# Ten byte offsets, modulo 512, for the weight buffers of a linear-attention and MLP kernel

## The chip, the cores and the metric

The kernel runs on one core of a Trainium2 chip. The metric is device time in microseconds of one execution: 1016.26 us before the change, the median of 2 runs (1016.14 to 1016.39).

## What is computed

The reference first runs attention with random features (8 batches, 8 heads, 576 tokens, head size 64, 128 features), and then a two-layer network over the 4608 tokens, 512 wide, with 2048 hidden units and softplus between the layers:

```python
def phi(x):
    proj = np.einsum('bhsd,md->bhsm', x, omega)
    h = proj - np.sum(x * x, axis=-1, keepdims=True) / 2.0
    h = h - np.max(h, axis=-1, keepdims=True)
    return np.exp(h) / np.sqrt(m)
q_p, k_p = phi(q * scale), phi(k * scale)
kv, z = einsum('bhsm,bhsd->bhmd', k_p, v), sum(k_p, axis=2)
x = einsum('bhsm,bhmd->bhsd', q_p, kv) / (einsum('bhsm,bhm->bhs', q_p, z)[..., None] + 1e-06)
x = x.transpose(0, 2, 1, 3).reshape(4608, 512)
h = x @ w_in                                        # 512 -> 2048
g = maximum(h, 0.0) + log1p(exp(-abs(h)))
out = g @ w_out                                     # 2048 -> 512
```

## The kernel before

The network takes nearly all of TensorE's time. Its tokens go in ten blocks: two of 256 tokens and eight of 512, the last of which (the `rest`) holds what the other blocks left over. The hidden units go in 16 chunks of 128 (`fc` 0 to 15). The numbers are split into a high and a low part, both float32r, and each product is made of three matmuls. Layer 1 (L923 to L925) multiplies a chunk of `w_in`, which is loaded into the array as the stationary operand (128 columns, 512 bytes of each partition), with 512 tokens of `xh` or `xl`, which stream through it (the moving operand, 2048 bytes of each partition). Layer 2 (L952 to L954) is the other way round: 128 tokens of `gh` or `gl` are loaded, and 512 columns of the chunk of `w_out` stream. A weight load is an instruction of its own in the trace (PEld), and the load for the next matmul runs while the present one streams.

Between the layers ScalarE and VectorE make softplus and the split (L929 to L946). The attention of later batches runs between the matmuls of the network: features (L399, L424), key-value sums (L563), and the normalised output (L865). Its projections in full float32 and its other float32 matmuls are called the side work below.

`in_order` is a list scheduler written in Python. It takes every piece of work with its cost and due time and writes the instructions of all engines in one order when the program is built. The same planner decides which numbered buffer a piece gets, by tag.

All 16 chunks of `w_in` and all 16 of `w_out` are kept in SBUF once they are made: 32 buffers with the tags `w.0` to `w.31`, each of 4096 bytes a partition. Such a buffer ends as the tile `wi<fc>` or `wo<fc>`, with the high part in its first 2048 bytes and the low part in the second. Before that the same buffers hold the first batch's keys and queries (`xk`, `xq`, loaded at L371 and L373, written over by their own features) and the weights as they come from memory (`rawi`, `rawo`, loaded at L274). L282 to L303 turn a raw buffer into the two parts of a weight buffer.

Tiles come from pools, and a pool lays its tiles one after the other in each partition. Before the change the 32 buffers are in the pool `const`, behind `xh`, `xl` and the small constants. All 32 begin at byte 192 modulo 512. So do `xh`, `xl`, `gh` and `gl`, and so does every slice that a matmul of the network reads, since the slices are multiples of 512 bytes apart.

Of the kernel before, what the change touches and what calls it, by code (L numbers as in the profile page):

```python
# [10 lines left out]
F32 = mybir.dt.float32  # L11
F32R = mybir.dt.float32r
U32 = mybir.dt.uint32
# [6 lines left out]
P = 128  # L20
# [4 lines left out]
DM = 512  # L25
# [162 lines left out]
def favor_softplus_kernel(ctx, tc, q0, k0, qx, kx, tx, vv, om, wi, wo, out):  # L188
# [5 lines left out]
            name=nc.get_next_instruction_name(), act_func_set_id=ACT_SET_LN_EXP,  # L194
# [4 lines left out]
    const = ctx.enter_context(tc.tile_pool(name="const", bufs=1))  # L199
    at = ctx.enter_context(tc.tile_pool(name="at", bufs=1))  # L200
    ff = ctx.enter_context(tc.tile_pool(name="ff", bufs=2))
    dram = ctx.enter_context(tc.tile_pool(name="dram", bufs=2, space=bass.MemoryType.DRAM))
    ps = ctx.enter_context(tc.tile_pool(name="ps", bufs=8, space=PSUM))

    def bank(name, tag):
        return ps.tile([P, 512], F32, name=name, tag=tag, bufs=1)

    idle = at.tile([P, P], F32, name="idle", tag="x.0", bufs=1)
    nc.vector.memset(idle, 0.0)
# [13 lines left out]
    f = ff.tile([P, 512], F32, name="omf1", tag="t2.0", bufs=1)[:, :M]  # L223
# [23 lines left out]
    def act(n, space=None):  # L247
        return (0.066 if space == PSUM else 0.105) + 0.000833 * n

    def dve(n, rate=1):  # L250
        return 0.068 + 0.001042 * n / rate

    def pool(n):
        return 0.06 + 0.00228 * n

    def do(engine, cost, due, emit, **kw):

        on = dict(zip(engine, cost)) if isinstance(engine, tuple) else {engine: cost}
        w = Work(on, due, emit, **kw)
        works.append(w)  # L260
        return w
# [3 lines left out]
    def plan_weights(nm, fc, due):  # L265

        src, w = (wi, w1) if nm == "i" else (wo, w2)
        last = fc == NFC - 1
        box = {}

        def load():

            t = (at if last else const).tile([P, 2 * DM], U32, name=f"raw{nm}{fc}", tag=box["raw"], bufs=1)
            nc.sync.dma_start(t, src[fc].bitcast(U32))  # L274
            box["words"], words = t, t.rearrange("p (c t) -> p c t", t=2)
            box["low"], box["high"] = words[:, :, 0], words[:, :, 1]

        def low_bits(e):

            low = box["low"]  # L280
            if e == "ACT":
                nc.scalar.activation(low.bitcast(I32), low, AF.Copy, scale=0.936 * 2.0**-29)  # L282
            else:
                nc.vector.tensor_scalar(low.bitcast(I32), low, 2.0**-29, 7.0, ALU.mult, ALU.min)

        def rebias():


            h = box["high"].bitcast(F32)
            nc.scalar.activation(h, h, AF.Prelu, scale=2.0**-112, alpha=2.0**32)  # L290

        def joined():
            box["all"] = box["words"][:, :DM].bitcast(F32)
            nc.vector.scalar_tensor_tensor(
                box["words"][:, :DM], box["high"], 3, box["low"], ALU.logical_shift_left, ALU.bitwise_or
            )

        def high_part(e):
            w[fc] = const.tile([P, 2, DM], F32R, name=f"w{nm}{fc}", tag=box["w"], bufs=1)
            (nc.vector.tensor_copy if e == "DVE" else nc.scalar.copy)(w[fc][:, 0], box["all"])  # L300

        def low_part(e):
            (nc.vector if e == "DVE" else nc.gpsimd).tensor_tensor(  # L303
                w[fc][:, 1], box["all"], w[fc][:, 0].bitcast(F32), ALU.subtract
            )

        l = do(
            "SP", 1.46, due + 8.41, load, delay=DL, spare=0 if last else 2,
            take=[({"i": "qh", "o": "ql"}[nm] if last else "w", box, "raw")],
        )  # L310
        aw, dw, dw2, pw = act(DM), dve(DM), dve(DM, 2), pool(DM)
        a = do(("ACT", "DVE"), (aw, dw2), due, low_bits, after=[l], port=True)
        b = do("ACT", aw, due, rebias, after=[l])
        c = do("DVE", dw, due, joined, after=[a, b], port=True)
        d = do(
            ("ACT", "DVE"), (aw, dw2), due, high_part, after=[c] + (in_w if last else []), take=[("w", box, "w")], port=True,
        )
        if not last:
            in_w.append(d)
        return do(("DVE", "POOL"), (dw, pw), due, low_part, after=[d], give=[(box, "raw")], port=True)  # L320
# [26 lines left out]
    def plan_unit(q, kind, us, due, early, other=None):  # L347

        u = us[0]
        nm = f"{kind}{q.nm}_{u}"  # L350
# [7 lines left out]
        w, n = nt * P, 2 * nt  # L358
        b = {}

        def load():
            if early:

                x = const.tile([P, 2 * DM], F32, name=f"x{nm}", tag=b["x"], bufs=1)
                b["v"] = x[:, UW : UW + 4 * (D + 1)].rearrange("p (c d) -> p c d", d=D + 1)
                b["qt"] = x[:, UW : UW + 4 * P].rearrange("p (c t) -> p c t", t=P)
                b["xs"] = x[:, : 4 * D]
                b["ph"] = x[:, : n * M].rearrange("p (c m) -> p c m", m=M)
                b["raw"], b["nat"] = x[:, :w], x[:, w : 2 * w].rearrange("p (c d) -> p c d", d=D)
                if kind == "k":  # L370
                    nc.sync.dma_start(x[:, :VW], src[:, u * VW : (u + 1) * VW])  # L371
                else:
                    nc.sync.dma_start(x[:, : 2 * w], src[:, u * UW : u * UW + 2 * w])  # L373
                return
            x = at.tile([P, 2 * UW], F32, name=f"x{nm}", tag=b["x"], bufs=1)
            nc.sync.dma_start(x[:, : 2 * w], tx[other.n - NQ] if other else src[:, u * UW : u * UW + 2 * w])
            b["raw"], b["nat"] = x[:, :w], x[:, w : 2 * w].rearrange("p (c d) -> p c d", d=D)
# [14 lines left out]
        def project():  # L392

            both = [bank(f"pp{nm}_{j}", b["ppb", j]) for j in range(2)]
            b["pp"] = [x[:, : nt * M].rearrange("p (t m) -> p t m", m=M) for x in both]
            for t in range(nt):
                for j in range(2):
                    r = slice(j * D, (j + 1) * D)
                    nc.tensor.matmul(  # L399
                        b["pp"][j][:, t], b["raw"][r, t * P : (t + 1) * P], omf[r],  # L400
                        start=True, stop=True,
                    )
# [18 lines left out]
        def product(t):  # L421
            b["pr", t] = bank(f"pp{nm}_{t}", b["ppb", t]).rearrange("p (j i m) -> p j i m", j=2, i=2)
            for j in range(2):
                nc.tensor.matmul(b["pr", t][:, j], b["sp"][:, j, t * P : (t + 1) * P], omr, start=True, stop=True)  # L424
# [38 lines left out]
        def exponent(j):  # L463
# [7 lines left out]
        size = P * 4 * (VW if early and kind == "k" else 2 * w)  # L471
        ld = do(
            "SP", dma(size), due - 2.45, load, behind=prev.get("load"),
            take=[("w" if early else "x", b, "x")], delay=DL, spare=2 if early else 0,
        )
# [73 lines left out]
    def plan_keys(q, us, due, b, es, early):  # L549
# [19 lines left out]
        def kv_bank():  # L569
            q.bank = bank(f"kt{q.nm}", q.slots["kt"])  # L570
            q.kvt = q.bank[:, : 2 * M].rearrange("p (j m) -> p j m", m=M)
# [639 lines left out]
```

## Time and profile before

| | |
|---|---|
| median of the runs | 1016.26 us |
| the profiled execution | 1014.9 us, of which the span from the first to the last instruction is 1013.1 us |
| TensorE clock that was granted | 0.998 |
| PE (matmuls) | 998.3 us busy, 99% of the span, 5752 matmuls |
| PEld (weight loads) | 809.0 us, 80% |
| DVE (VectorE) | 742.7 us, 73% |
| ACT (ScalarE) | 659.7 us, 65% |
| POOL (GpSimd) | 119.1 us, 12% |

A row for a group of instructions names the line, the engine, the operation, the tiles written and read, the shape and the count. Behind the bar stand the busy time, the mean duration of one in ns, the idle time before, and what ended it. The end of a matmul is modelled and its record reaches into the next one's, so that a 512-column matmul is recorded with some 390 ns. What one costs in a stream is the distance from its start to the next one's start.

### The profile page before, as it was taken

The page shows a single profiled execution, that of the slowest core. Times are in us where ns is not written, and L with a number is a line of the kernel's source. Part 1 is how long each engine was busy: PE and PEld are TensorE (multiplying, and loading weights), DVE is VectorE, ACT ScalarE, POOL GpSimd, SP SyncE. Part 2 cuts the span into 40 slices and gives each one's busy share as a digit, 9 for nine tenths or more (in the row PEclk, how much of TensorE's full clock was granted, in tenths as well). Part 3 has the DMA queues.
Part 4 walks back from the last instruction along what each step waited for, and adds up shares of the span by engine and source line. Part 5 has one row for each costly group of instructions (what it writes and reads, how often), then busy time and mean ns, then how long its engine had stood idle before and what let it go on. Part 6 is the DMA issues. An engine that isn't in the chain of part 4 may idle for free.

```text
span 1013.1 us, 17023 instructions
## 1 busy us (share of the span) xinstructions
PE 998.3 (99%) x5752; PEld 809.0 (80%) x5752; DVE 742.7 (73%) x2027; ACT 659.7 (65%) x1592; POOL 119.1 (12%) x125
## 2 busy tenths in 40 slices
PE   9999999999999999999999999999999999999997
PEld 8888788877777787878787777778788778888885
DVE  6999988988888787878787887878797733222222
ACT  6999977767666675756576666667575645444442
POOL 2212221010021010110112011211011100000000
PEclk9999999999999999999999999999999999999999
DMA  9774344433442424343333333352533121001001
GB/s 345 305 265 176 116 151 126 150 114 101 121 145 72 133 84 141 115 128 97 120 126 102 113 94 110 96 149 73 152 115 89 54 75 54 1 1 42 1 1 42
DMA packets 64175, 113.82 MB, mean 112 GB/s; under 512 B 18236, under 2 KB 36824, under 8 KB 64088
## 3 DMA queue, kind: packets, MB, share of 16 engines
q1 hardware_dynamic: 64088, 112.73, 35.0%
q8 instruction: 46, 0.75, 0.3%
q14 instruction: 41, 0.34, 0.1%
HBM read 85.68 MB, written 27.03 MB: 111 GB/s over the span
## 4 chain that ended last, share of the span: by engine, by line
PE 87%; DVE 6%; ACT 4%; DMA 2%; issue 1%; POOL 0%; SPq 0%; DVEq 0%
PE acc L952 13%; PE h L923 12%; PE acc L953 12%; PE acc L954 12%; PE h L924 12%; PE h L925 12%; PE ppk L399 3%; PE xp L865 3%; PE kt L563 3%; PE ppq L424 2%; DMA xk<-kx 1%; DVE junk L785 1%; PE fill L1103 1%; DMA xq<-qx 1%; ACT xq L469 0%
## 5 line engine op out<-in xcount | busy, mean ns | idle before, releaser
L923 PE MATMUL h<-xh,wi 128*128 128x512 f32 (+1 forms) x640 | 239.5, 374 | 1.4 <-DVE u L938 1.4
L924 PE MATMUL h<-xl,wi 128*128 128x512 f32 (+1 forms) x640 | 236.0, 369 | 0.0
L925 PE MATMUL h<-xh,wi 128*128 128x512 f32 (+1 forms) x640 | 235.6, 368 | 0.0
L952 PE MATMUL acc<-wo,gh 128*128 128x512 f32 x576 | 231.1, 401 | 0.5 <-ACT kvs L581 0.5
L953 PE MATMUL acc<-wo,gh 128*128 128x512 f32 x576 | 225.4, 391 | 0.0
L954 PE MATMUL acc<-wo,gl 128*128 128x512 f32 x576 | 224.8, 390 | 0.2 <-DVE gl L946 0.2
L929 ACT ACTIVATE u<-h 128x512 f32<-128x512 f32 (+1 forms) x160 | 89.2, 558 | 168.2 <-PE h L925 160.1
L938 DVE SCALAR_TENSOR_TENSOR u<-h,u 128x512 f32<-128x512 f32 (+1 forms) x160 | 101.2, 633 | 119.5 <-ACT u L935 117.7
L923 PEld LDWEIGHTS h<-xh,wi 128*128 128x128 f32 x640 | 120.5, 188 | 29.6 <-issue 5.4
L925 PEld LDWEIGHTS h<-xh,wi 128*128 128x128 f32 x640 | 120.5, 188 | 20.6
L924 PEld LDWEIGHTS h<-xl,wi 128*128 128x128 f32 x640 | 120.5, 188 | 19.0
L952 PEld LDWEIGHTS acc<-wo,gh 128*128 128x128 f32 x576 | 108.1, 188 | 29.9 <-issue 7.2
L954 PEld LDWEIGHTS acc<-wo,gl 128*128 128x128 f32 x576 | 108.1, 188 | 24.1 <-DVE gl L946 0.6
L953 PEld LDWEIGHTS acc<-wo,gh 128*128 128x128 f32 x576 | 108.4, 188 | 18.0
L942 ACT CAST gh<-u 128x512 fp32r<-128x512 f32 (+1 forms) x122 | 71.4, 585 | 57.1 <-PE acc L953 52.7
L946 DVE TENSOR_TENSOR gl<-u,gh 128x512 fp32r<-128x512 f32 (+1 forms) x128 | 85.4, 667 | 26.2 <-ACT gh L942 24.7
L935 ACT ACTIVATE u<-u 128x512 f32<-128x512 f32 (+1 forms) x160 | 94.4, 590 | 4.8
L932 ACT ACTIVATE u<-u 128x512 f32<-128x512 f32 (+1 forms) x160 | 94.6, 591 | 3.9
L785 DVE CUSTOM_DVE_ANT_0 junk<-phq,zb 128x128 bf16<-128x128 f32 (+1 forms) x228 | 79.1, 347 | 17.6 <-ACT phq L446 1.7
L794 POOL TENSOR_TENSOR phq<-phq,dnq 128x512 f32<-128x512 f32 (+1 forms) x43 | 45.9, 1071 | 209.9 <-DVE dnq L790 129.8
L946 POOL TENSOR_TENSOR gl<-u,gh 128x512 fp32r<-128x512 f32 (+1 forms) x32 | 36.2, 1130 | 280.9 <-ACT gh L942 148.3
L469 ACT ACTIVATE phk<-ppk,smk 128x128 f32<-128x128 f32 x230 | 63.8, 377 | 2.6 <-DVE smk L461 1.3
(129 smaller groups left out, 1293.3 us busy)
## 6 DMA issues: line engine op xcount, KB each, us to landing
xk<-kx SPq DMA_DIRECT2D x28, 512.0 KB
xq<-qx SPq DMA_DIRECT2D x28, 512.0 KB
fdq<-flq SPq DMA_DIRECT2D x28, 512.0 KB
qq<-fdq SPq DMA_DIRECT2D x112, 128.0 KB
rawi<-wi SPq DMA_DIRECT2D x16, 512.0 KB
rawo<-wo SPq DMA_DIRECT2D x16, 512.0 KB
out<-o SPq DMA_DIRECT2D x32, 256.0 KB
v<-vv SPq DMA_DIRECT2D x14, 576.0 KB
```

The lines of the kernel that those rows point to most:

```text
L785: nc.vector.tensor_tensor_reduce(jk[r, c % jk.shape[1]], ph[r, c], q.zb[r, h], 1.0, 1e-6, ALU.mult, ALU.add, dn[r, 0, c : c + 1])
L923: nc.tensor.matmul(b["h"], wh, xh[:, cc, t], start=cc == 0, stop=False)
L924: nc.tensor.matmul(b["h"], wh, xl[:, cc, t], start=False, stop=False)
L925: nc.tensor.matmul(b["h"], wl, xh[:, cc, t], start=False, stop=cc == NCC - 1)
L929: nc.scalar.activation(b["u"], b["h"], AF.Abs)
L932: nc.scalar.activation(b["u"], b["u"], AF.Exp, scale=-1.0)
L935: nc.scalar.activation(b["u"], b["u"], AF.Ln, bias=1.0)
L938: nc.vector.scalar_tensor_tensor(b["u"], b["h"], 0.0, b["u"], ALU.max, ALU.add)
L946: (nc.vector if e == "DVE" else nc.gpsimd).tensor_tensor(b["gl"], b["u"], b["gh"].bitcast(F32), ALU.subtract)
L952: nc.tensor.matmul(acc[tt], gh, w2[fc][:, 0], start=fc == 0, stop=False)
L953: nc.tensor.matmul(acc[tt], gh, w2[fc][:, 1], start=False, stop=False)
L954: nc.tensor.matmul(acc[tt], gl, w2[fc][:, 0], start=False, stop=fc == NFC - 1)
```

## The change

The 32 buffers get a pool of their own, `ws`, that is opened last and so lies behind the other pools. A helper, `big`, makes each of the 32 on its first use. Before the 4th, 7th, 10th, and so on up to the 28th of them it first takes a gap tile of 32 bytes a partition.

```diff
     ff = ctx.enter_context(tc.tile_pool(name="ff", bufs=2))
+    ws = ctx.enter_context(tc.tile_pool(name="ws", bufs=1))
...
+    placed = []
+
+    def big(shape, dtype, name, tag):
+        if tag not in placed:
+            if placed and len(placed) % 3 == 0 and len(placed) < 30:
+                ws.tile([P, 8], F32, name=f"gap{len(placed)}", tag=f"gap{len(placed)}", bufs=1)
+            placed.append(tag)
+        return ws.tile(shape, dtype, name=name, tag=tag, bufs=1)
...
-            t = (at if last else const).tile([P, 2 * DM], U32, name=f"raw{nm}{fc}", tag=box["raw"], bufs=1)
+            n = f"raw{nm}{fc}"
+            t = at.tile([P, 2 * DM], U32, name=n, tag=box["raw"], bufs=1) if last else big([P, 2 * DM], U32, n, box["raw"])
...
-            w[fc] = const.tile([P, 2, DM], F32R, name=f"w{nm}{fc}", tag=box["w"], bufs=1)
+            w[fc] = big([P, 2, DM], F32R, f"w{nm}{fc}", box["w"])
...
-                x = const.tile([P, 2 * DM], F32, name=f"x{nm}", tag=b["x"], bufs=1)
+                x = big([P, 2 * DM], F32, f"x{nm}", b["x"])
```

In the built program the buffers then begin at these bytes modulo 512, in the order of their first use, with the weights that they hold at the end:

| offset | weights | offset | weights |
|---|---|---|---|
| 192 | wo13, wo6, wo14 | 352 | wi6, wo11, wo5 |
| 224 | wi14, wi3, wo8 | 384 | wi0, wo12, wi12 |
| 256 | wo1, wi4, wi9 | 416 | wi13, wo7, wi1 |
| 288 | wo15, wo3, wi8 | 448 | wi15, wo9, wi10 |
| 320 | wo4, wi5, wo2 | 480 | wo10, wi2, wi11, wi7, wo0 |

All other tiles of the pools `at` and `ff` and the `kvs` tiles move down by 131072 bytes, so that they keep their place modulo 512; `xh`, `xl` and the tiles ahead of them do not move. The instructions of every engine, their order, the waits, and which buffer each of them uses are the same before and after. Only addresses differ.

## The prediction

> **What bounds the kernel now.** I read the page first, then the stretches of the span, then the groups of matmuls, and last the single matmuls in order of time, because an address can only act through the duration of an instruction.
>
> ```profile
> span 1013.1 us, 17023 instructions
> ...
> PE 998.3 (99%) x5752; PEld 809.0 (80%) x5752; DVE 742.7 (73%) x2027; ACT 659.7 (65%) x1592; POOL 119.1 (12%) x125
> ...
> PE 87%; DVE 6%; ACT 4%; DMA 2%; issue 1%; POOL 0%; SPq 0%; DVEq 0%
> ```
>
> The chain that ended last is 87% TensorE. The view of the busy time in three stretches (columns: microseconds, then busy time and count of PE, PEld, DVE, ACT and POOL) shows where that holds.
>
> ```profile
> 0.00:80.00 80.00, 74.94 (x634) 64.25 (x635) 70.56 (x230) 69.36 (x192) 15.25 (x23) 1.00 0.81 302
> 80.00:830.00 750.00, 747.17 (x4343) 599.14 (x4343) 620.08 (x1717) 508.27 (x1262) 103.80 (x102) 1.00 0.37 115
> 830.00:1010.00 180.00, 176.24 (x778) 145.61 (x776) 52.10 (x82) 82.03 (x139) 0.00 (x0) 1.00 0.06 20
> ```
>
> From 80 us on TensorE is busy for 99.4% of the time. The other engines have slack there (VectorE 620 of 750 us), so that the time is the sum of the distances between matmul starts. Ahead of 80 us VectorE and ScalarE are nearly as busy as TensorE, and DMA runs at 0.81 of its engines; there a slower transfer or a slower vector instruction would show as well.
>
> The groups of 512-column matmuls by shape are the part that the change can reach. Of the 3264, layer 1 has 1536, and all read a weight buffer as their weight load; layer 2 has 1728 that stream one.
>
> ```profile
> L952 PE MATMUL acc<-wo,gh 128*128 128x512 f32 x576 | 231.1, 401 | 0.5 <-ACT kvs L581 0.5
> L953 PE MATMUL acc<-wo,gh 128*128 128x512 f32 x576 | 225.4, 391 | 0.0
> L954 PE MATMUL acc<-wo,gl 128*128 128x512 f32 x576 | 224.8, 390 | 0.2 <-DVE gl L946 0.2
> L923 PE MATMUL h<-xh,wi 128*128 128x512 f32 x512 | 201.9, 394 | 0.0
> L924 PE MATMUL h<-xl,wi 128*128 128x512 f32 x512 | 199.9, 390 | 0.0
> L925 PE MATMUL h<-xh,wi 128*128 128x512 f32 x512 | 199.5, 390 | 0.0
> ```
>
> What is the undisturbed distance between two starts? The last block runs without side work: the stretch from 850 to 1000 us, and two of its six groups.
>
> ```profile
> 850.00:1000.00 150.00, 150.00 (x664) 124.20 (x663) 40.36 (x60) 69.16 (x114) 0.00 (x0) 1.00 0.02 8
> ...
> L952 PE MATMUL acc<-wo,gh 128*128 128x512 f32 x114 | 44.3, 389 | 0.0
> ...
> L925 PE MATMUL h<-xh,wi 128*128 128x512 f32 x108 | 42.0, 389 | 0.0
> ```
>
> 664 matmuls touch these 150 us; 150 us over 662 whole ones is 226.6 ns, and all six groups have the same recorded 389 ns. It makes no difference whether the weight buffer is loaded (L925) or streamed (L952), though ScalarE is busy for 69 us and VectorE for 40 us of this stretch, reading and writing the same memory.
>
> Just behind a change from side work to the network the distance is not constant. TensorE's matmuls in order of time, at about 475 us (start, recorded duration):
>
> ```profile
> 475.20 0.50 PE L952 MATMUL acc<-wo,gh 128*128 128x512 f32 x1
> 475.54 0.40 PE L953 MATMUL acc<-wo,gh 128*128 128x512 f32 x1
> 475.78 0.40 PE L954 MATMUL acc<-wo,gl 128*128 128x512 f32 x1
> 476.01 0.40 PE L952 MATMUL acc<-wo,gh 128*128 128x512 f32 x1
> 476.25 0.40 PE L953 MATMUL acc<-wo,gh 128*128 128x512 f32 x1
> 476.48 0.39 PE L954 MATMUL acc<-wo,gl 128*128 128x512 f32 x1
> 476.71 0.39 PE L952 MATMUL acc<-wo,gh 128*128 128x512 f32 x1
> 476.94 0.40 PE L953 MATMUL acc<-wo,gh 128*128 128x512 f32 x1
> 477.18 0.39 PE L954 MATMUL acc<-wo,gl 128*128 128x512 f32 x1
> 477.40 0.40 PE L424 MATMUL ppk<-omr,spk 128*128 128x256 f32 x2
> ```
>
> The second starts 0.24 us ahead of the third, 13.4 ns over the steady value; the eight from 475.54 to 477.40 take 0.2325 us each, 5.9 ns over it. So something between a stream and the load beside it can cost up to 13 ns a matmul, and the question is whether the byte distance of the two, modulo 512, is part of it.
>
> **The change part by part.** Nothing is removed, added or moved on any engine; the instructions, their order, their waits and the queues are identical, so no new wait can arise except through a duration. The gap tiles hold 288 bytes a partition and no instruction touches them. What changes is the distance, modulo 512, between the two operands of a matmul: from 0 to something from 32 to 288 bytes for all 1536 of layer 1, and for 13 of 16 chunks of layer 2, 1404 of 1728, since wo6, wo13 and wo14 stay at 192. That makes 2940 matmuls of 512 columns (and 384 of 256 columns, of layer 1 in the first two blocks).
>
> _Term 1, the steady distance of the 2940._ The rows do not show a network matmul at another distance, so I bound it. The worst settled value would be the worst in the rows, 13.4 ns more each: 2940 x 13.4 ns = 39 us. The other end takes as much below: -39 us. Which value? A weight load that follows a change of work shows how fast it reads (weight loads in order of time, same place):
>
> ```profile
> 475.20 0.19 PEld L952 LDWEIGHTS acc<-wo,gh 128*128 128x128 f32 x1 [0.39 <-issue]
> 475.31 0.19 PEld L953 LDWEIGHTS acc<-wo,gh 128*128 128x128 f32 x1
> ```
>
> The second load starts 0.11 us behind the first, with nothing to wait for but the first load; so a load passes its 512 bytes in about 110 ns, while a matmul streams its 2048 bytes in 227 ns and so passes 1000 bytes meanwhile. The stream thus runs ahead of the load by about 490 of 512 bytes during every load. Wherever the two begin, their distance modulo 512 passes through nearly all values once. Whatever collisions there are should be as many at any starting distance. Beside that stands the last stretch: two other engines at arbitrary phases leave 389 ns in all six groups. Memory in which streams collide by address should show some of that. I take the value 0.
>
> [...]
>
> _Term 2, the unsettled matmuls after a change of work._ The excess of the recorded durations over 389 ns holds them all: 576 x (12 + 2 + 1) ns + 512 x (5 + 1 + 1) ns = 12.2 us. Of this the first matmul of a run, which waits for its own load (0.50 us at 475.20, 0.11 more than steady), is no matter of addresses; the side work of L865 alone, 28 times, is followed by such a one, 28 x 0.11 = 3.1 us. That leaves 9 us: -9 us if another distance settled at once, +9 if it took twice as long. I take 0, the order of work being the same.
>
> _Term 3, vector work on the buffers, ahead of 80 us for the most part._ Groups of the same width, on moved and unmoved tiles:
>
> ```profile
> L946 DVE TENSOR_TENSOR gl<-u,gh 128x512 fp32r<-128x512 f32 x109 | 77.4, 711 | 25.6 <-ACT gh L942 24.3
> L636 DVE TENSOR_TENSOR s<-s,phk 128x512 f32<-128x512 f32 x28 | 20.5, 730 | 1.5
> L294 DVE SCALAR_TENSOR_TENSOR rawi<-rawi 128x512 uint32<-128x512 uint32 x16 | 10.9, 684 | 0.0
> L294 DVE SCALAR_TENSOR_TENSOR rawo<-rawo 128x512 uint32<-128x512 uint32 x16 | 10.9, 683 | 0.0
> L303 DVE TENSOR_TENSOR wo<-rawo,wo 128x512 fp32r<-128x512 f32 x13 | 8.9, 681 | 0.0
> L303 DVE TENSOR_TENSOR wi<-rawi,wi 128x512 fp32r<-128x512 f32 x12 | 8.2, 682 | 0.1
> ```
>
> The same shape takes 681 to 730 ns, 7% apart, with all tiles at the same offset. 7% of VectorE's 38.9 us on the weights is 2.7 us, to either side if it all were in the way. I take 0.
>
> _Term 4, the loads into the buffers._ The two busiest stretches for DMA:
>
> ```profile
> 0.00:20.00 20.00, 18.55 (x148) 16.04 (x150) 11.93 (x52) 11.41 (x36) 3.96 (x12) 1.00 0.91 333
> 20.00:40.00 20.00, 18.54 (x161) 16.07 (x161) 19.70 (x67) 19.12 (x54) 4.43 (x6) 1.00 1.03 405
> ```
>
> At equal share of the engines they moved 366 and 393 GB/s, 7% apart by kind of transfer. 7% of 40 us is 2.8 us; behind that DMA is at 0.37 and has slack. I take 0: the bytes and the rows of a transfer are the same, and so is their start modulo 32.
>
> **The sum** is 0: 1014.9 us for the profiled execution again. The median of the runs stands 1.4 us above that execution, so I forecast 1016.3 us.
>
> **The rivals.**
>
> _Faster: the common offset is what makes a stream slow._ If the settled 226.6 ns hold a collision that another distance avoids, as large as the one that the rows show on top of it (13.4 ns), then 2940 x 13.4 = 39 us go, and with half of it on 384 matmuls of 256 columns 2.6 more: 975 us. If only half of the offsets help, 996 us, which is just 2%. For it speaks that the swing at 475 us is TensorE's own; against it the distance that runs through all values in every load, and that TensorE's distances are the same for layer 1 and layer 2. [...]
>
> _Slower: the equal offsets are what lets the stream settle._ The run behind 475.54 settles at 226.6 ns. With another distance it may never do so: the mean of those eight, 5.9 ns over, on 2940 matmuls gives 17 us, 1033 us; at the worst of them always, 1055 us. It decides for over 2% (20.3 us) from 6.9 ns a matmul on. For it speaks that a settled state exists at all, which needs some fixed relation; against it the same as above.
>
> _The change acts only ahead of 80 us._ Terms 3 and 4 then give up to 5.5 us to either side: 1011 to 1022 us, and the verdict of no change.
>
> **How the numbers follow.** A measurement of this kernel tells about 2% from no change. No effect beyond terms 2 to 4, the third rival included: 0.85, with a time within 1007 to 1026 us (term 2's 9 us to either side, terms 3 and 4 not all at one end with it). The faster rival: 0.08, of which 0.06 beyond 2%. The slower one: 0.07, of which 0.05 beyond 2%. So 0.06 faster, 0.89 within 2%, 0.05 slower. The range is that of the likeliest case, which leaves out 0.15.
>
> **What would show it.** In the profile after, the stretch 850 to 1000 us should again hold 663 or so matmuls of 389 ns in all six groups. Different recorded means for layer 1 and layer 2, or fewer nanoseconds where wi is loaded, would show the faster rival; a spread of 391 to 402 ns in that stretch the slower one. Term 2 is right if L952 stays at about 401 and L923 at 394 ns over the whole span; term 3 if L294 and L303 keep 681 to 684 ns; term 4 if the first 40 us still move 330 to 405 GB/s. The prediction is wrong if the load reads faster than its records say, so that it keeps step with the stream: then the starting distance decides in each matmul, for better or worse.

## The result: 1029.13 us, 1.1% slower

The changed kernel takes 1029.13 us (median of 2 runs, 1029.03 to 1029.23) against 1016.26 us, a ratio of 1.0112 (95% interval 1.0087 to 1.0137). The profiled execution took 1029.23 us with a span of 1027.5 us, 14.4 us more than before. The forecast of 1016.3 us, and its range of 1007 to 1026 us, were wrong.

The functions stand eleven lines lower: layer 1 is now L934 to L936, layer 2 L963 to L965. The groups of 512-column matmuls over the whole span, after the change:

```profile
L963 PE MATMUL acc<-wo,gh 128*128 128x512 f32 x576 | 233.0, 405 | 0.5 <-ACT kvs L592 0.5
L965 PE MATMUL acc<-wo,gl 128*128 128x512 f32 x576 | 227.3, 395 | 0.0
L964 PE MATMUL acc<-wo,gh 128*128 128x512 f32 x576 | 227.1, 394 | 0.0
L934 PE MATMUL h<-xh,wi 128*128 128x512 f32 x512 | 203.8, 398 | 0.0
L935 PE MATMUL h<-xl,wi 128*128 128x512 f32 x512 | 201.8, 394 | 0.0
L936 PE MATMUL h<-xh,wi 128*128 128x512 f32 x512 | 201.8, 394 | 0.0
```

All six are 3 to 5 ns longer than before: 576 x (4 + 3 + 5) ns + 512 x (4 + 4 + 4) ns = 13.1 us, about the whole change of 12.9 us in the medians. Taken matmul by matmul, the distances from one 512-column matmul to the next account for some 12.2 of the span's 14.4 us; 1.5 of the rest is one place at 673 us, where a matmul of the side work (L435) waits for VectorE and the next start comes after 1.58 us instead of 0.11. The kernel with all weights at 192, below, has the same wait and yet the time of before.

The last stretch, which has no side work, is where it is read best:

```profile
850.00:1000.00 150.00, 150.00 (x648) 121.34 (x647) 41.11 (x63) 69.06 (x117) 0.00 (x0) 1.00 0.04 15
```

648 matmuls instead of 664 in 150 us, with ScalarE and VectorE as idle as before (busy for 69.06 and 41.11 us, against 69.16 and 40.36) and the clock granted at 1.00. Two chunks in a row there, by TensorE's matmuls in order of time (start, recorded duration), show it: layer 1 of chunk 10 begins at 978.86 (wi10, at 448), layer 2 of chunk 7 at 981.58 (wo7, at 416), and the next chunk at 984.38.

```profile
978.86 0.39 PE L934 MATMUL h<-xh,wi 128*128 128x512 f32 x1
...
981.58 0.40 PE L963 MATMUL acc<-wo,gh 128*128 128x512 f32 x1
...
984.38 0.40 PE L934 MATMUL h<-xh,wi 128*128 128x512 f32 x1
```

Twelve matmuls with the weights 256 bytes from the other operand take 2.72 us, 226.7 ns each, as before the change. Twelve with the weights 224 bytes away take 2.80 us, 233.3 ns each. The changed kernel thus holds its own comparison, chunk by chunk. The table has, from its trace from 150 us on, the mean time from the start of a 512-column matmul to that of the float32r matmul right behind it (times of 250 ns and more, behind an interruption, are left out). It is grouped by the byte distance, modulo 512, from the stream's first byte to that of the next matmul's weight load, with the number of pairs in brackets. Before the change all 2992 pairs have distance 0, with 228.0 ns; after it, all 2990 together have 232.2.

| distance | ns | distance | ns | distance | ns | distance | ns |
|---|---|---|---|---|---|---|---|
| 0 | 230.4 (394) | 128 | 232.4 (77) | 256 | 228.0 (281) | 384 | 232.4 (172) |
| 32 | 232.8 (184) | 160 | 233.7 (93) | 288 | 233.1 (353) | 416 | 233.5 (175) |
| 64 | 233.4 (176) | 192 | 231.3 (173) | 320 | 233.5 (97) | 448 | 233.3 (95) |
| 96 | 233.5 (90) | 224 | 233.4 (360) | 352 | 233.6 (170) | 480 | 233.3 (100) |

Only 256 comes close to the value of before. The group at 0 holds many pairs right behind a chunk at another distance, and 192 follows with 231.3.

The single times from start to start tell more than these means, for where no side work falls between they repeat from block to block to within a nanosecond or two (chunk 7 of layer 2, at distance 288, begins with 234 or 235, 235, 231 or 232, 235 ns in each of the last six blocks). In the last block chunk 6 of layer 2, at distance 0, begins with 236, 224, 231, 235, 229, 232, 231 ns and then stays at 226 to 227. Chunks at other distances run into other patterns there: chunk 5 of layer 1, at 128, has 229 and 237 to 238 ns in turn, and chunk 12, at 192, ends with 226, 229, 232 ns twice over (another chunk at 192 stays at 233). The steady 226 to 227 ns are reached at 0 and 256 alone.

### The profile page after: what moved, and what is told of

Read it like the earlier page. It is cut to its first block, busy times and chain, and to the rows that moved or that the text cites. A ratio compares the mean times of both kernels' runs of the same rounds, so it can differ in the third digit from the quotient of the medians.

```text
span 1027.5 us, 17023 instructions
## 1 busy us (share of the span) xinstructions
PE 1011.2 (98%) x5752; PEld 808.6 (79%) x5752; DVE 743.8 (72%) x2027; ACT 659.5 (64%) x1592; POOL 118.6 (12%) x125
## 4 chain that ended last, share of the span: by engine, by line
PE 85%; DMA 6%; DVE 5%; ACT 2%; issue 1%; SPq 0%; DVEq 0%
PE acc L963 13%; PE h L934 12%; PE acc L964 12%; PE h L935 12%; PE acc L965 12%; PE h L936 12%; PE xp L876 3%; PE kt L574 3%; PE ppk L410 3%; PE ppq L435 2%; DMA xq<-q 2%; DMA xk<-kx 1%; DVE junk L796 1%; DMA xq<-qx 1%; DMA rawi<-wi 1%
## 5 line engine op out<-in xcount | busy, mean ns | idle before, releaser
L934 PE MATMUL h<-xh,wi 128*128 128x512 f32 (+1 forms) x640 | 241.3, 377 | 1.5 <-DVE u L949 1.4
L936 PE MATMUL h<-xh,wi 128*128 128x512 f32 (+1 forms) x640 | 237.6, 371 | 0.0
L963 PE MATMUL acc<-wo,gh 128*128 128x512 f32 x576 | 233.0, 405 | 0.5 <-ACT kvs L592 0.5
L965 PE MATMUL acc<-wo,gl 128*128 128x512 f32 x576 | 227.3, 395 | 0.0
L934 PEld LDWEIGHTS h<-xh,wi 128*128 128x128 f32 x640 | 120.2, 188 | 32.0 <-issue 5.4
L936 PEld LDWEIGHTS h<-xh,wi 128*128 128x128 f32 x640 | 120.2, 188 | 22.6
L963 PEld LDWEIGHTS acc<-wo,gh 128*128 128x128 f32 x576 | 108.2, 188 | 31.4 <-issue 7.4
L965 PEld LDWEIGHTS acc<-wo,gl 128*128 128x128 f32 x576 | 108.2, 188 | 26.0 <-DVE gl L957 0.5
```

The costliest lines, as they stand in the source:

```text
L934: nc.tensor.matmul(b["h"], wh, xh[:, cc, t], start=cc == 0, stop=False)
L936: nc.tensor.matmul(b["h"], wl, xh[:, cc, t], start=False, stop=cc == NCC - 1)
L963: nc.tensor.matmul(acc[tt], gh, w2[fc][:, 0], start=fc == 0, stop=False)
L965: nc.tensor.matmul(acc[tt], gl, w2[fc][:, 0], start=False, stop=fc == NFC - 1)
```

## The experiments

Theory A: the distance between a weight load and the stream beside it decides, modulo 256. Its rivals: B, the place of the buffers in memory; C, the change of offset from buffer to buffer; D, the stream's own start; E, the place of both within 256 bytes. A ratio is always to runs of the kernel before that were taken along with those of the experiment. All kernels but those on what the load adds do the full computation with the same instructions in the same order; only addresses differ.

**All weights at one offset.** From the changed kernel:

```diff
-            if placed and len(placed) % 3 == 0 and len(placed) < 30:
-                ws.tile([P, 8], F32, name=f"gap{len(placed)}", tag=f"gap{len(placed)}", bufs=1)
+            if not placed:
+                ws.tile([P, 64], F32, name="gap0", tag="gap0", bufs=1)
```

These lines are those for 448; for 224 the gap is `[P, 8]`, and for 192 the two lines are taken out and nothing is put in.

> The weights' own pool without the gaps: all 32 buffers in their new place, 62464 bytes higher in each partition, but all at 192 modulo 512 like xh, xl, gh and gl. If the distance between a weight load and the stream beside it is what costs (theory A), the time is that of before, 1016 us, and the last stretch has 389 ns again. If the place of the buffers in memory costs (theory B), it is 1029 us.

> All 32 buffers at 448 modulo 512, 256 bytes from the other operands. In the changed kernel the chunks at 448 alone had 226.7 to 227.3 ns from start to start in the last block. If the distance counts modulo 256 (theory A), 1016 us and 389 ns. If any distance other than 0 modulo 512 costs some 5 ns (A with modulo 512), 3264 matmuls x 5 ns more than before: 1033 us. If it is the change of offset from buffer to buffer that unsettles the stream (theory C), 1016 us.

> All 32 buffers at 224 modulo 512, 32 bytes from the other operands, one offset for all. Theory A: each of the 3264 matmuls of 512 columns costs what the chunks at 224 cost in the changed kernel, 233.0 ns in layer 1 and 233.4 in layer 2 against 227.8 and 228.4 before: 1536 x 5.2 + 1728 x 5.0 ns = 16.6 us more, 1033 us. Theory C (the change of offset from buffer to buffer): 1016 us. Theory D (a stream that begins off a multiple of 64 bytes costs, that is layer 2 alone): 8.7 us more, 1025 us, and layer 1 as before.

**The other operands moved instead.** From the kernel before, with the weights left in their pool at 192 modulo 512 (`gl` moves in the same way as `gh`):

```diff
+    mv = ctx.enter_context(tc.tile_pool(name="mv", bufs=1))
...
-    xh = const.tile([P, NCC, RING], F32R, name="xh")
-    xl = const.tile([P, NCC, RING], F32R, name="xl")
+    mv.tile([P, 8], F32, name="gap0")
+    xh = mv.tile([P, NCC, RING], F32R, name="xh")
+    xl = mv.tile([P, NCC, RING], F32R, name="xl")
...
-            b["gh"] = ff.tile([P, TB], F32R, name=f"gh{nm}", tag="gh" + b["gs"], bufs=1)[:, :n]
+            b["gh"] = mv.tile([P, TB], F32R, name=f"gh{nm}", tag="gh" + b["gs"], bufs=1)[:, :n]
```

> The weights stay as before the change, in their old pool at 192; instead xh, xl, gh and gl get a pool of their own, behind the others, at 224 modulo 512. Theory A: the distances are as with all weights at 224, with the other sign: 1033 us. Theory B (the place of the weights) and theory C: 1016 us. Theory D (the stream's own start): layer 1 alone slower, 1024 us.

| kernel | distance modulo 512, layer 1 and layer 2 | median us | ratio to before, 95% interval |
|---|---|---|---|
| all at 192 | 0, 0 | 1016.44 | 1.0000 (0.9985 to 1.0014) |
| all at 448 | 256, 256 | 1015.62 | 0.9994 (0.9983 to 1.0005) |
| all at 224 | 32, 480 | 1030.89 | 1.0152 (1.0133 to 1.0172) |
| xh, xl, gh, gl at 224 | 480, 32 | 1030.09 | 1.0143 (1.0127 to 1.0159) |

The stretch from 850 to 1000 us of the four, in this order:

```profile
850.00:1000.00 150.00, 150.00 (x664) 124.20 (x663) 39.64 (x59) 70.50 (x116) 0.00 (x0) 1.00 0.02 8
```
```profile
850.00:1000.00 150.00, 150.00 (x663) 124.20 (x662) 39.41 (x59) 69.12 (x114) 0.00 (x0) 1.00 0.02 8
```
```profile
850.00:1000.00 150.00, 150.00 (x645) 120.65 (x644) 40.95 (x63) 68.40 (x115) 0.00 (x0) 1.00 0.04 15
```
```profile
850.00:1000.00 150.00, 150.00 (x644) 120.67 (x643) 40.79 (x63) 68.34 (x114) 0.00 (x0) 1.00 0.04 15
```

The third count is what tells: 664 and 663 at distance 0 and 256, 645 and 644 at 32 and 480. B falls, for the weights moved by 62464 bytes cost nothing, and 32 bytes more cost 1.5%. (The last kernel does not have its weights exactly where they were, as the expectation says: `xh` and `xl` have left the pool ahead of them, and they lie 32768 bytes lower, still at 192 modulo 512.) C falls, for one offset for all costs no less than ten. D falls: within the chunks, from start to start, layer 1 has 227.8 ns and layer 2 228.4 before the change. With the weights at 224 both are slower, layer 1 (whose stream has not moved) at 233.0 ns and layer 2 at 233.2, and with the others at 224 the two have 233.2 and 233.1. Both slow kernels came out 2 to 3 us under the 1033 us that A gave.

**Both operands moved together.** The kernel before with a gap of 64 bytes ahead of `xh`.

```diff
+    const.tile([P, 16], F32, name="gap0")
     xh = const.tile([P, NCC, RING], F32R, name="xh")
```

> The kernel before with a gap of 64 bytes ahead of xh: weights, xh, xl, gh, gl and everything behind them begin at 256 modulo 512, so that all distances between a load and the stream beside it stay 0 and only the place itself moves. Theory A (the distance alone counts): 1016 us and 389 ns in the last block. Theory E (the place within 256 bytes counts as well): another settled duration than 389 ns, and some microseconds to either side for each ns (3264 matmuls: 3.3 us a ns).

Measured: 1016.09 us, ratio 1.0003 (0.9986 to 1.0019), and in the last stretch:

```profile
850.00:1000.00 150.00, 150.00 (x664) 124.24 (x663) 39.83 (x60) 70.44 (x116) 0.00 (x0) 1.00 0.02 8
```

E falls as well, for this one other place; of the theories on the addresses the distance alone is left.

**Distances between the steps of 32.** The changed kernel with a gap before every fourth buffer, and `xh` and `xl` in one padded tile of a pool of their own, 16 bytes (shown) or 4 bytes (`1 + i` in place of `4 + i`) behind a step of 32.

```diff
+    mv = ctx.enter_context(tc.tile_pool(name="mv", bufs=1))
...
-            if placed and len(placed) % 3 == 0 and len(placed) < 30:
+            if placed and len(placed) % 4 == 0:
...
-    xh = const.tile([P, NCC, RING], F32R, name="xh")
-    xl = const.tile([P, NCC, RING], F32R, name="xl")
+    xx = mv.tile([P, 2 * NCC * RING + 8], F32R, name="xx")
+    xh, xl = (
+        xx[:, 4 + i * NCC * RING : 4 + (i + 1) * NCC * RING].rearrange("p (c t) -> p c t", t=RING)
+        for i in range(2)
+    )
```

> The weights at eight offsets 32 bytes apart, four buffers at each, and xh and xl together 16 bytes off that grid, so that the distances of layer 1 are 16, 48, 80 and so on modulo 256; layer 2 has 0, 32, 64 and so on. Theory A with streams that collide over a stretch of memory: the distances in between cost what their neighbours cost, 231 to 234 ns, with 16 and 240 between these and 226.6; 1028 to 1030 us. If collisions are a matter of single 16-byte lines, some of these distances may settle lower than 226.6 ns, which would be the way to a faster kernel.

> As the run before, with xh and xl 4 bytes off the grid: layer 1 has the distances 28, 60, 92 and so on modulo 256 (the same as 4 bytes short of a step of 32). Expected as at the neighbouring steps of 32, 231 to 234 ns, and close to 226.6 at 4 bytes short of 0: 1028 to 1030 us. [...]

One run each: 1028.65 and 1036.39 us. At 16 bytes off the grid, layer 1 has means of 230.0 to 233.8 ns by chunk offset; no distance comes below the 227.8 ns of layer 1 before the change, so there is no better place among them. That answers the question of the faster kernel with no, for the multiples of 16 that this run has. At 4 bytes off, layer 1 has 235.4 to 237.6 ns, about 5 more, at each distance. Expected were the values of the neighbouring steps of 32, and close to 226.6 ns next to distance 0, where it measured 236.0. Something about the 4 bytes costs, then, at every distance. It may be the stream's own start inside 16 bytes or the distance, which is no multiple of 16 either; this kernel changes both at once and does not tell them apart. The groups of layer 1 in the last stretch of that kernel, with 389 before:

```profile
L939 PE MATMUL h<-xx,wi 128*128 128x512 f32 x108 | 43.1, 399 | 0.0
L940 PE MATMUL h<-xx,wi 128*128 128x512 f32 x108 | 43.0, 399 | 0.0
L938 PE MATMUL h<-xx,wi 128*128 128x512 f32 x108 | 43.0, 398 | 0.0
```

**What the load adds.** Are the settled 226.6 ns a stream plus its collisions with the load (theory A, carried further), or the price of the stream itself (theory F)? By the first a lighter load makes the stream faster, by how much no run had shown; by the second it leaves the settled value as it is. The kernel before with loads that read less (the first column 128 times; in the second kernel the 33rd):

```diff
-                wh, wl = (w1[fc][:, s, cc * P : (cc + 1) * P] for s in range(2))
+                wh, wl = (w1[fc][:, s, cc * P : cc * P + 1].broadcast_to([P, P]) for s in range(2))
...
-            gh, gl = (b[k][:, tt * P : (tt + 1) * P] for k in ("gh", "gl"))
+            gh, gl = (b[k][:, tt * P : tt * P + 1].broadcast_to([P, P]) for k in ("gh", "gl"))
```

> The kernel before, but each weight load of both layers reads the first of its 128 columns 128 times (a step of zero) and so touches 4 bytes of a partition instead of 512; the output is no longer the reference's. [...] If 226.6 ns are the price of streaming 512 columns of this type, and loads only ever add to it (theory F), the last block keeps 389 ns and only the unsettled matmuls get shorter: 1007 to 1016 us.

> Each load reads the 33rd of its 128 columns 128 times, which lies 128 bytes behind the first. A standing load is passed by the stream at every distance, eight times in 2048 bytes if the period is 256, so that its place should not matter (theory A): 231.1 ns again on average, 1024 us. If the place of a standing load counts like that of a moving one, another value between 226.6 and 234 ns.

The first took 1024.76 us, ratio 1.0081 (1.0063 to 1.0099), the second 1025.75 us in one run. The last stretch of each:

```profile
850.00:1000.00 150.00, 150.00 (x649) 122.30 (x648) 38.99 (x58) 68.31 (x114) 0.00 (x0) 1.00 0.03 11
```
```profile
850.00:1000.00 150.00, 150.00 (x650) 122.26 (x649) 39.32 (x59) 68.60 (x114) 0.00 (x0) 1.00 0.03 11
```

Both theories missed: a load that touches 4 bytes instead of 512 makes the stream slower (231.2 and 231.6 ns on average), not faster and not the same. The place of that element makes little difference, as A said: in the last stretch both kernels have 231.7 ns.

For the next two, layer 2 loads 32 columns instead of 128, and the 32 rows that come out are copied and stored four times, so that a few instructions of other engines change too; the second has all weights at 224 besides.

```diff
-            gh, gl = (b[k][:, tt * P : (tt + 1) * P] for k in ("gh", "gl"))
-            nc.tensor.matmul(acc[tt], gh, w2[fc][:, 0], start=fc == 0, stop=False)
+            gh, gl = (b[k][:, tt * P : tt * P + 32] for k in ("gh", "gl"))
+            nc.tensor.matmul(acc[tt][:32], gh, w2[fc][:, 0], start=fc == 0, stop=False)
...
```

> The kernel before, but layer 2 loads only the first 32 of each 128 tokens (128 bytes of a partition instead of 512), so that its output holds 32 rows of each 128, four times; layer 1 is as before. [...] If 226.6 ns are the price of the stream itself (theory F), layer 2 keeps 226.6 ns and 389 ns in the last block.

> The same with all weights at 224 modulo 512, so that the distance is 32 in both layers. Layer 1 with its full loads should have 233 ns again. Layer 2: if the collisions happen all along a load, a quarter of the load leaves a quarter of the 5 ns, some 1.2 ns over what layer 2 has at distance 0; if the distance at the start alone puts the stream into another state, the whole 5 ns stay.

Measured: 1024.58 and 1029.38 us, one run each, beside one of the kernel before with 1015.15. Layer 2 of the first, in the last stretch, and its layer 1:

```profile
L954 PE MATMUL acc<-wo,gl 128*32 128x512 f32 x109 | 42.9, 394 | 0.0
...
L924 PE MATMUL h<-xl,wi 128*128 128x512 f32 x108 | 42.5, 394 | 0.0
L923 PE MATMUL h<-xh,wi 128*128 128x512 f32 x108 | 42.5, 393 | 0.0
L925 PE MATMUL h<-xh,wi 128*128 128x512 f32 x108 | 41.9, 388 | 0.0
```

Again neither theory: a quarter of the load leaves layer 2 at 231.1 ns instead of 228.4, and layer 1, whose loads were not touched, goes to 230.0. Its trace shows where this comes from: each chunk of layer 1 in the last block begins behind an unsettled layer 2 and runs through 234, 236, 224, 231, 235, 229, 232, 231 ns before it is at 226 to 227. With the weights at 224 layer 2 has 231.7 ns, so that with short loads the distance costs 0.6 ns and not 5. That fits an effect along the length of a load better than one of the start alone, but does not show it, since layer 2 is unsettled in both kernels. Of all the kernels here only the full load of 512 bytes at distance 0 or 256 lets the stream settle at 226.6 ns. Everything else, less load included, has means of 230 to 238.

These loads also give the pace of a load. In order of time, with 32 and with 128 columns:

```profile
899.90 0.11 PEld L953 LDWEIGHTS acc<-wo,gh 128*32 128x32 f32 x1
...
900.37 0.19 PEld L923 LDWEIGHTS h<-xh,wi 128*128 128x128 f32 x1
```

By these records 96 columns, 384 bytes, take 0.08 us, which makes 512 bytes in some 107 ns, an estimate from these two lines.

## Why the prediction was wrong, by its own steps

**What bounds the kernel** was right (though its two rows from 80 us on give 99.3%, not 99.4): from 80 us on the time is the sum of the distances between matmul starts, and 13.1 us in the six groups gave 12.9 us in the median.

**Term 1** is the step that failed. It had bounds of 39 us to either side and took 0, because a load passes 512 bytes while the stream passes 1000, so that all distances should come by in each load wherever it begins. The runs show the start deciding: +14 us (1.5%) at a start of 32 bytes, none at 256. The pace was not the error: the loads of 32 columns give an estimate of 107 ns for 512 bytes, next to the 110 of the prediction, so by these records the load does not keep step with the stream, and the way of being wrong that the prediction names last did not come about. What failed is the step from "all distances come by" to "as many collisions at any start". It takes each matmul by itself, at a fixed pace; but the rows around 475 us, at distance 0, are a row of matmuls on its way into a settled pattern, in which a matmul's time depends on those before it (layer 1 went from 227.8 to 230.0 ns when the loads of layer 2 alone were shortened). Whether the row gets to 226.6 ns goes with the distance: it does at 0 and 256, and at no other distance that was tried. I read those rows as a swing to be bounded and not as what the whole kernel could turn into. The second reason, that ScalarE and VectorE leave all groups at 389 ns, is still true and says nothing on TensorE's two own streams.

**Terms 2 to 4.** Term 2 can't be told from term 1 any more, since nearly all matmuls are off the settled value now; its sign, L952 at 401 and L923 at 394 ns, did not hold (405 and 398). Terms 3 and 4 held to within a microsecond. VectorE's work on the weights went from 684 and 683 to 713 and 686 ns (L305, before L294), 0.5 us in all, the subtraction (L314, before L303) stayed at 683, and the early transfers kept their rate:

```profile
L305 DVE SCALAR_TENSOR_TENSOR rawi<-rawi 128x512 uint32<-128x512 uint32 x16 | 11.4, 713 | 0.0
L305 DVE SCALAR_TENSOR_TENSOR rawo<-rawo 128x512 uint32<-128x512 uint32 x16 | 10.9, 686 | 0.0
```
```profile
0.00:20.00 20.00, 18.36 (x150) 15.81 (x150) 12.37 (x52) 11.54 (x36) 3.96 (x12) 1.00 0.91 333
20.00:40.00 20.00, 18.53 (x160) 16.06 (x159) 19.68 (x67) 18.92 (x54) 4.39 (x6) 1.00 1.03 406
```

**The rivals.** The slower one was the mechanism: equal offsets let the stream settle. I gave it 0.07, and 5.9 ns on 2940 matmuls, 17 us. The matmuls are now at 232.2 ns, 5.6 over the settled 226.6, so the size was nearly right; but the kernel before stood at 228.0 on average, and only 4.2 ns are new. The 17 us counted the unsettled matmuls of before a second time. The chunks at 448 are as good as before, which I missed because I counted every distance but 0 as another one; the steps of 32 pass through 256. The faster rival is refuted for the distances tried: none of them, and no lighter load, brought 512 columns of float32r below 226.6 ns in a settled row of matmuls.

**What stays open.** That the distance decides is shown; why the row settles at 226.6 ns at equal starts, and what a stream at 231 to 234 ns waits for, was not found. That short and standing loads are slow as well speaks against a plain count of bytes that collide. There is no run without any load, since each matmul brings its own (5752 of either in the page of before).

## What to carry to other kernels

When TensorE is the bound and its matmuls run back to back, compare the start-to-start distance in a quiet stretch with that behind every kind of interruption: two values for one instruction (here 226.6 ns and, behind side work, 232.5) mean that something decides between them, and an edit that looks neutral can move all of them to the worse one. For float32r matmuls of 512 columns with loads of 128, keep the first byte of the load and that of the stream beside it equal modulo 256 (226.6 ns against 231 to 234), and begin both at multiples of 16 bytes (a stream 4 bytes behind one took 235.4 to 237.6 ns; no other start inside 16 bytes was tried). Whether the same holds for other types and shapes was not tried. An argument that something averages out over an instruction needs a row in which the average is seen; without one, both ends of the bound belong in the range.

## What the runs showed of the hardware that was not expected

- The distance between a weight load's first byte and the stream's, modulo 256, changes a 512-column float32r matmul from 226.6 ns (at 0 and at 256) to 231 to 234 ns from start to start; sign, layer and absolute place make less than 1 ns where they were tried (32 bytes to either side, 233.0 to 233.2 ns; both operands moved by 64 bytes, 226.6).
- A lighter load is not faster: 128 reads of one element give 231.2 ns, 32 columns instead of 128 give 231.1 ns, at the distance at which the full load settles at 226.6 ns.
- A stream that begins 4 bytes behind a multiple of 16, beside loads that begin at such a multiple, took about 5 ns more in one run (235.4 to 237.6 ns against 230.0 to 233.8); whether its own start or the distance costs this was not told apart.
- A matmul's duration depends on those before it: layer 1 rose from 227.8 to 230.0 ns when its own loads and streams stayed as they were and those of layer 2 were shortened; it needed eight matmuls to come back to 226 to 227 ns.
- A load of 128 columns passes its 512 bytes in some 107 ns, an estimate from the records of loads of 32 (0.11 us) and 128 columns (0.19 us).
